# One table for the order of a first up-projection stage (RetNet recurrence, then a SwiGLU block, in fp32 on one core)

## The chip, the core and the metric

The kernel runs on one core of one Trainium2 chip. The metric is the device time of one execution in microseconds (us); lower is better. A core has five engines with a queue each: TensorE (PE, whose weight loads are listed as PEld), VectorE (DVE), ScalarE (ACT), GpSimd (POOL) and SyncE (SP), which here issues every DMA.

## The reference

```python
def _attn_ref(q, k, v):                       # (B,H,S,D) = (4, 8, 768, 64)
    gamma = 1.0 - 2.0 ** (-5.0 - np.arange(H))
    for t in range(S):
        state = gamma[None, :, None, None] * state + einsum('bhd,bhe->bhde', k[:, :, t], v[:, :, t])
        y[:, :, t] = scale * einsum('bhd,bhde->bhe', q[:, :, t], state)

def _moe_ref(x, w_gate, w_val, w_out):        # (3072,512), (512,1536) twice, (1536,512)
    g = x @ w_gate
    silu = g * (1.0 / (1.0 + np.exp(-g)))
    return silu * (x @ w_val) @ w_out

x = attn_out.transpose(0, 2, 1, 3).reshape(B * S, H * D)
return _moe_ref(x, w_gate, w_val, w_out)
```

The three weight matrices arrive as float64 words and are turned into float32 on the chip.

## The kernel before, in words

**Tiling.** The sequence is cut into chunks of 128 positions, and the 24 chunks of all batches are worked in four segments of six chunks (`seg_chunks`; three positions of two sequences). For each segment there is an attention part (scores, mixing, states), an "up" stage (12 blocks `f` of 128 columns of d_ff, gate and value) and a "down" stage (12 blocks times 6 groups of tokens). The attention of segment s+1 is threaded into the down stage of segment s (`down_stage`).

**The first segment is different.** Its attention runs ahead of everything, in the order of the string given to `do(...)` near the end of the kernel. In that string `s` is the scores of a chunk on PE with two masking multiplications on DVE (L356, L362), `m` the mixing (L413, L416) with a copy by ACT (L419), `t` the state update on PE (L396), `g` the decay of the state on ACT (L382), `k`/`q` the scaling of keys and queries on POOL (capital letters: on DVE), `x` the four operand sums on DVE, `w` warm-up products with no result. `scores` takes its two PSUM banks from one pair, 4 and 5, for every chunk, so a chunk's scores cannot be written before the masking of the chunk before has read those banks.

The up stage of the first segment (`up(f)`, L601 on PE) forms the gate and value products with seven products per block in a Strassen-like scheme, each of four matmul records of 128x384 in fp32. Beside them, in the same stage, everything is prepared that the later segments reuse. For each of 24 weight pieces (12 up, then 12 down): a load of raw words (`load_piece`: `U`, L194), the steps `a`, `b`, `c` on ACT (L212, L216, L220), `S` on DVE (L226) and `C` on POOL (L235). For an up piece then `T`, three differences on DVE, and a store of the unit to DRAM (L160). For a down piece then `F` with parts 0 to 3: ACT (L667), POOL (L670), DVE (L673), DVE (L677), which fill one of three `oitem` tiles, and a store (L252).

**What sets the order.** Each block `f` has six places, at which `aside(f, place)` emits side work between two products. Engines run their own instructions in the order of emission, and so does the DMA queue of SP. Before the change the side work of a place comes from three sources: the dictionary `beside`, filled from formulas (`when`, `loads_at`, `todo`), a list `stores` (each store goes out at the start of the place after the one that made it), and events in time (`at`/`run`), which hold the side tables and the first transfers for the next segment:

```python
for i in range(4):
    at(T0 + UP0 * (5.3 + i / 2), load_side, i // 2, i % 2)
for n in range(5):
    at(T0 + UP0 * (7.5, 8.2, 8.8, 9.5, 10.2)[n], load_pair, 1, n)
```

`load_side(g, m)` (L436, L438, L442) brings a half of a side table for the later segments into `tab` (g = 0) or `kept_vk` (g = 1); `load_pair` (L452, L455) brings keys, queries and values. The two gate multiplications of block f-1 (`muls`, L616 and L617 on DVE) stand at a fixed spot in `up(f)`, ahead of the first sum of the block (L633). The transposed loads `U` of pieces share places: the up pieces 2, 5, 8, 11 use the first `rawp` tile, 1, 4, 7, 10 the second, 3, 6, 9 the third; the down pieces use halves of the fourth and of `loads`.

Of the kernel before, what the change touches and what calls it, by code (L numbers as in the profile page):

```python
# [13 lines left out]
U32 = mybir.dt.uint32  # L14
# [35 lines left out]
def tile_retnet_swiglu(  # L50
# [88 lines left out]
    def load_chunk(c, places):  # L139
        for t in places:  # L140
            own = chunks.setdefault(c, [])
            nc.sync.dma_start(out=t, in_=(k_t, q_t, v_n, k_n)[len(own)][c])
            own.append(t)
# [26 lines left out]
    def load_piece(piece):  # L170
# [11 lines left out]
        if wide:  # L182
            t = raw_places[kind].pop(0)
            if kind == "down" or a:
                raw_places[kind].append(t)
            to = raw[piece] = t.bitcast(U32).rearrange("p (a b) -> p a b", a=n)
# [10 lines left out]
    places, stores = [0], []  # L197
# [41 lines left out]
    def three_dn(piece, part):  # L239
        a = piece[1]  # L240
        if part == 0:
            wo[a] = item("o", DM)
        o, x = [wo[a][:, i] for i in range(3)], made[DOWN.index(a) % 5]
        if part == 0:
            far_a(o, x)
        elif part == 1:
            far_b(o, x, pool)
        elif part == 2:
            far_c(o)
        else:  # L250
            far_d(o, True)
            stores.append((places[0], lambda: nc.sync.dma_start(  # L252
                out=w_dn3[a], in_=wo[a].bitcast(U32))))

    def sums_t(piece, parts=range(3)):
# [9 lines left out]
        if parts[-1] == 2:  # L265
            stores.append((places[0], lambda: keep_wt(a)))
# [13 lines left out]
        "U": lambda n: load_next("up"), "D": lambda n: load_next("down"),  # L280
        "F": lambda n, p: three_dn(pieces[n], p[0]),
# [3 lines left out]
    def do(order):  # L285
        for o in order.split():
            n, _, part = o[1:].partition(":")
            parts[o[0]](int(n or 0), *([[int(part)]] if part else []))

    beside = {  # L290
        (0, 0): "c1 S1 C1 U D", (0, 2): "a2 b2", (0, 3): "c2", (0, 5): "T1",
        (1, 0): "a3", (1, 1): "S2 b3 C2 U", (1, 2): "c3", (1, 4): "T2", (1, 5): "S3 C3 U",
    }

    when = [(4, 14, 15, 16, 16, 16), (12, 9, 9, 10, 11, 11, 17, 18)]
    when += [(f + 2, *(6 * f + i for i in (-3 + (f == 3), -2 + (f == 3), -1, 1, 1))) for f in range(3, 10)]
    when += [(f + 10, *(6 * f + i for i in (2, 2, 3, 3, 3, 5, 6))) for f in range(3, 9)]
    when += [(f + 19, *(54 + 2 * f + i for i in (0, 0, 1, 1, 1, 5, 6))) for f in range(5)]
    loads_at = [(16, "U")] + [(6 * f + 1, "U") for f in range(3, 7)]
    loads_at += [(q, "D") for q in (12, 18, 24, 30, 36, 42, 46, 47, 48)]  # L300
    sign_banks.update({3: (4, 6), 12: (7,), 19: (4,), 20: (7,), 21: (6,), 22: (7,), 23: (6,)})
    todo = [(6 * n - 7 if n > 4 else 6 * n - 4 + (n == 3), f"T{n}") for n in range(3, NF)]
    todo += [(53, "k4"), (59, "k5"), (61, "t4"), (66, "t5")]
    for n, *at_ in when:
        sign_banks.setdefault(n, (6, 7) if n < NF else (4,))
        ops = [f"{p}{n}" for p in "abcSC"] + [f"F{n}:0 F{n}:1", f"F{n}:2 F{n}:3"]
        todo += zip(at_, ops)
    order = lambda e: (e[0], "CUD".find(e[1][0]))
    for q, what in sorted(todo + loads_at, key=order):
        key = divmod(q, 6)  # L310
        beside[key] = beside.get(key, "") + " " + what

# [3 lines left out]
    def aside(f, place):  # L316
        places[0] = 6 * f + place
        while stores and (stores[0][0] <= places[0] - 1):
            stores.pop(0)[1]()
        if (f, place) == (7, 5):  # L320
            raw_places["down"][:0] = [hsp[:, ts(i, 1024)] for i in range(2)]
        do(beside.get((f, place), ""))
        run(T0 + UP0 * (f + (place + 1) / 7))

    to_load = {"up": [("up", f) for f in range(NF)], "down": [("down", f) for f in DOWN]}

    raw_places = {"up": [loadp[0][:, :2048], loadp[1][:, :2048], loadp[0][:, :2048],
                         hsp[:, :2048]],
                  "down": [midp[:, ds(0, 1024)], midp[:, ds(1024, 1024)],
                           loads[:, ds(0, 1024)], loads[:, ds(1024, 1024)]]}  # L330

    def load_next(kind):
        if to_load[kind]:
            load_piece(to_load[kind].pop(0))
# [15 lines left out]
    def scores(c):  # L350
        kt, qt = (pairs(t) for t in chunks[c][:2])
# [33 lines left out]
    def state(c):  # L385
# [3 lines left out]
        vn, kd = chunks[c][2:]  # L389
# [44 lines left out]
    def load_side(g, m):  # L434
        cols = decays[:, MASK0:QDEC0].rearrange("p (i g t) -> p i g t", i=2, g=2)[:, :, g]
        nc.sync.dma_start(out=side[g][half[m], :, : 2 * P], in_=cols[half[0]])  # L436
        for i in range(2):
            nc.sync.dma_start(  # L438
# [152 lines left out]
    def up(f):  # L591
# [39 lines left out]
        if f:  # L631
            left.pop(f - 1)[1]()
# [84 lines left out]
    def make_x(t, s, p):  # L717
        soon = p == L - 1
        for m in range(4):
            at(t + 0.4 * m, sum_x, m)  # L720
        when = [(0.2, 1.7, 2.3, 3.0), (0.9, 2.6, 3.0, 3.4), (1.6, 3.5, 4.3, 5.4)] if soon else [
            (0.2, 2.0, 2.6, 3.4), (0.9, 3.2, 3.6, 4.2), (1.6, 3.9, 6.6, 8.0)]
        for (a, b, c, d), n in zip(when, (1, 2, 0)):
            at(t + a, lambda n=n: far_a(*x_part(s, p, n)))
            at(t + b, lambda n=n: far_b(*x_part(s, p, n)))
            at(t + c, lambda n=n: far_c(x_part(s, p, n)[0]))
            at(t + d, lambda n=n: far_d(x_part(s, p, n)[0]))
# [21 lines left out]
    def weights(t, f, g):  # L749
        it = {}  # L750
        if f == 0:
            t -= 1.8
# [5 lines left out]
        at(t - 7.2, begin)  # L758
        at(t - 5.6, lambda: near_b(*it["o"]))
        at(t - 4.4, lambda: near_c(it["o"][0]))  # L760
# [11 lines left out]
    def up3(s, f, t):  # L772
# [9 lines left out]
        e = lambda n: t + (n + 1) * PROD + 0.1  # L782
        at(e(0), copy, p1, x)
        at(e(1), tt, c11, z, p1, op=add)
        at(e(1) + 0.7, act, gate, c11, AF.Silu, scale=ONE)
        at(e(2), copy, u2, x)
        at(e(3), copy, p5, wb)
        at(e(4), tt, hT[:, f, 1], x, p5, op=add)
        at(e(5), tt, hT[:, f, 0], wb, u2, op=add)
        at(e(5) + 0.7, tt, hT[:, f, 0], hT[:, f, 0], gate, op=mul)  # L790
        at(e(6), act, x, x, AF.Silu, scale=ONE)
        at(e(6) + 0.7, tt, hT[:, f, 1], hT[:, f, 1], x, op=mul)
# [5 lines left out]
    def h_split(t, f):  # L798
# [7 lines left out]
        at(t - 7.5, begin)  # L806
        at(t - 6.3, lambda: near_b(it["o"], hT[:, f].rearrange("p i t -> p (i t)")))
        at(t - 5.3, lambda: near_c(it["o"], both))
# [38 lines left out]
    def down_stage(s, t, first_order=range(6), between=None):  # L847
        nxt = s + 1 if s + 1 < NSEG else None
        slot_at, steps = [], []
        for n in range(6 * NF):  # L850
# [4 lines left out]
            if nxt and n in PARTS:  # L855
# [3 lines left out]
                if what == "s":  # L859
                    at(t, scores_of, p, g)  # L860
                    for i in range(2):
                        at(d, decayed, p, g, i)
                    if g and ci:
                        for i in range(2):
                            at(d, scale_q2, p, i)
                elif what == "m":
                    at(t, mix_own, nxt, p)
                    at(d, fence)
                    if ci < NCK - 1:
                        for i in range(2):  # L870
                            at(d, scale_k2, p, i)
                elif what == "o":
# [3 lines left out]
                    for c in range(2):  # L876
                        for i in range(2):
                            for hh in range(2):
# [149 lines left out]
```

## Time and profile before

| what | value |
|---|---|
| time, median of 3 runs | 697.34 us (695.87 to 697.41) |
| the profiled execution: time, span | 697.91 us, 696.1 us |
| granted TensorE clock, mean over the span | 0.994 |
| PE busy | 667.5 us, 96% of the span |
| DVE, ACT, POOL busy | 472.3 us, 383.3 us, 248.9 us |
| first matmul record of the first up stage (L601) | 29.05 us |
| last four records of L601 begin | 154.04 us |
| DMA moved over the span | 141.59 MB, mean 203 GB/s |

Times inside a profile count from the start of the span. The columns of a timeline are: start, length, engine, line, operation, tiles, how many records, and in brackets how long the engine had sat idle before it and what it waited for. "x <- y" in a list of waits reads: the engine and line named first waited for the one named after the arrow. PE is busy nearly everywhere, so the places where it is not, and what it waits for there, matter more than shares of busy time.

### The profile page before, as it was taken

What the parts mean: (1) busy time and instruction counts of PE and PEld (TensorE: products, weight loads), DVE (VectorE), ACT (ScalarE), POOL (GpSimd) and SP (SyncE); (2) the same over time, 40 slices, a digit from 0 to 9 for tenths busy, and PEclk for the clock granted to TensorE, in tenths of its full rate; (3) what the DMA queues carried; (4) which work ended last, traced back from release to release, by engine and by line L of the source; (5) the groups of instructions that cost most, each with busy time, mean ns of one, the idle gap of its engine ahead of it and who ended that gap; (6) DMA issues with size and microseconds to landing.
All of it is one profiled execution on the core that took longest, in us unless ns stands there. A gap on an engine that the chain in (4) does not pass through costs nothing.

```text
span 696.1 us, 12337 instructions
## 1 busy us (share of the span) xinstructions
PE 667.5 (96%) x4724; PEld 549.0 (79%) x4724; DVE 472.3 (68%) x742; ACT 383.3 (55%) x793; POOL 248.9 (36%) x164
## 2 busy tenths in 40 slices
PE   7998999979999999999999899999999999999997
PEld 7754555447677899997677799998777799999886
DVE  3766878955887766665776866666577867667541
ACT  2668689535565555553578554565464655545111
POOL 0434556620111665650100566651011455662000
PEclk9999999999999999999999999999999999999999
DMA  9799959964674543274766443354756553413553
GB/s 319 265 379 319 380 189 345 405 269 152 228 228 176 196 144 121 97 231 149 255 203 228 147 169 106 106 189 158 238 180 209 208 188 113 153 54 106 195 196 139
DMA packets 49515, 141.59 MB, mean 203 GB/s; under 512 B 6064, under 2 KB 18864, under 8 KB 49456
## 3 DMA queue, kind: packets, MB, share of 16 engines
q1 hardware_dynamic: 49456, 140.80, 58.3%
q8 instruction: 37, 0.61, 0.4%
q14 instruction: 22, 0.18, 0.1%
HBM read 114.04 MB, written 26.74 MB: 202 GB/s over the span
## 4 chain that ended last, share of the span: by engine, by line
PE 59%; DVE 17%; ACT 8%; issue 3%; DMA 3%; POOL 0%; DVEq 0%; ACTq 0%; POOLq 0%; SPq 0%
PE bank L768 34%; PE bank L820 14%; PE bank L601 7%; PE bank L458 4%; ACT chunk_x L699 3%; DVE gitem L661 3%; DMA wdnt<-oitem 2%; DVE x L673 2%; DVE x L80 2%; DVE gitem L80 1%; DVE tmp L80 1%; ACT gitem L658 1%; DVE hT L121 1%; DVE tmp L477 1%; DVE chunk_x L831 1%
## 5 line engine op out<-in xcount | busy, mean ns | idle before, releaser
L768 PE MATMUL bank<-x,gitem 128*128 128x384 f32 x1296 | 234.3, 336 | 4.6 <-ACT tmp L121 4.6
L768 PEld LDWEIGHTS bank<-x,gitem 128*128 128x128 f32 x1296 | 225.5, 188 | 8.4 <-ACT tmp L121 7.6
L820 PE MATMUL bank<-oitem,gitem 128*128 128x512 f32 x864 | 214.6, 401 | 0.7 <-DVE gitem L80 0.6
L820 PEld LDWEIGHTS bank<-oitem,gitem 128*128 128x128 f32 x864 | 158.7, 188 | 41.7 <-issue 2.9
L664 POOL TENSOR_TENSOR gitem<-gitem 128x768 fp32r<-128x768 f32 x72 | 136.0, 1889 | 133.7 <-DVE gitem L661 133.7
L601 PE MATMUL bank<-first 128*128 128x384 f32 x336 | 115.1, 501 | 8.5 <-DVE hT L617 3.6
L661 DVE SCALAR_TENSOR_TENSOR gitem<-gitem,loads 128x768 fp32r<-128x768 f32 x72 | 74.1, 1030 | 63.1 <-ACT gitem L658 63.1
L601 PEld LDWEIGHTS bank<-first 128*128 128x128 f32 x336 | 64.1, 194 | 57.5 <-issue 7.4
L661 DVE SCALAR_TENSOR_TENSOR gitem<-gitem,hT 128x768 fp32r<-128x768 f32 x48 | 46.3, 964 | 48.2 <-ACT gitem L658 48.2
L531 POOL TENSOR_TENSOR loads<-loads,tab 128x512 f32<-128x512 f32 x8 | 15.0, 1878 | 157.3 <-PE bank L458 157.3
L658 ACT ACTIVATE gitem<-loads 128x768 fp32r<-128x768 f32 x72 | 60.8, 844 | 0.0
L121 ACT ACTIVATE bank<-bank 128x384 f32<-128x384 f32 x36 | 17.1, 475 | 78.2 <-PE bank L768 78.2
L235 POOL TENSOR_TENSOR first<-first,rawp 128x1024 int32<-128x1024 int32 (+1 forms) x21 | 40.0, 1908 | 42.2 <-DVE first L226 12.7
L658 ACT ACTIVATE gitem<-hT 128x768 fp32r<-128x768 f32 x48 | 39.6, 837 | 25.9 <-PE bank L820 25.8
L121 ACT COPY tmp<-bank 128x384 f32<-128x384 f32 x108 | 51.2, 476 | 2.2 <-PE bank L768 1.9
L121 DVE TENSOR_TENSOR hT<-bank,tmp 128x384 f32<-128x384 f32 x72 | 39.6, 554 | 16.4 <-PE bank L768 16.4
L699 ACT COPY chunk_x<-bank 64x256 f32<-64x256 f32 x72 | 26.5, 368 | 37.4 <-PE bank L458 35.9
L80 DVE SCALAR_TENSOR_TENSOR gitem<-gitem 128x768 fp32r<-128x768 f32 x48 | 45.8, 955 | 1.0
L768 PE MATMUL bank<-x,oitem 128*128 128x384 f32 x216 | 43.9, 339 | 1.3 <-DVE hT L121 1.3
L121 ACT ACTIVATE bank<-tmp 128x384 f32<-128x384 f32 x36 | 17.8, 496 | 48.5 <-DVE tmp L121 48.5
L121 DVE TENSOR_TENSOR hT<-hT,bank 128x384 f32<-128x384 f32 x72 | 39.9, 554 | 4.9 <-ACT bank L121 1.6
L679 ACT ACTIVATE x<-x 128x512 fp32r<-128x512 f32 (+2 forms) x27 | 18.9, 700 | 37.8 <-DVE x L673 37.8
(89 smaller groups left out, 683.3 us busy)
## 6 DMA issues: line engine op xcount, KB each, us to landing
oitem<-wdnt SPq DMA_DIRECT2D x45, 768.0 KB, 4.3
loads<-wup SPq DMA_DIRECT2D x36, 896.0 KB, 4.7
wup<-first SPq DMA_DIRECT2D x12, 896.0 KB, 7.9
wdnt<-oitem SPq DMA_DIRECT2D x12, 768.0 KB, 8.2
rawp<-in_w_val_dram SPq DMA_DIRECT2D x24, 256.0 KB, 5.8
rawp<-in_w_gate_dram SPq DMA_DIRECT2D x12, 512.0 KB, 7.3
out_dram<-chunk_x SPq DMA_DIRECT2D x24, 256.0 KB, 2.1
loads<-in_k_t_dram SPq DMA_DIRECT2D x18, 256.0 KB, 4.2
```

Source lines behind the costliest of these rows:

```text
L80: stt(o, x, 1.0, y, op0=mul, op1=op)
L121: events.append((t, len(events), lambda: fn(*args, **kw)))
L235: pool(d[:, ts(i, n)].bitcast(I32), d[:, ts(i, n)].bitcast(I32), lo[:, ts(i, n)].bitcast(I32), op=add)
L458: nc.tensor.matmul(o, a, b, start=start, stop=True, skip_group_check=True)
L601: nc.tensor.matmul(o, w[:, slot, k], a[:, k], start=(start and k == 0), stop=(stop and k == KH - 1), skip_group_check=True)
L658: act(o[0], x, AF.Copy, scale=CUT / FAR)
L661: stt(o[1], f32(o[0]), -FAR, x, op0=mul, op1=add)
L664: op(o[2], f32(o[0]), f32(o[1]), op=add)
L679: act(o[2], f32(o[2]), AF.Copy, scale=FAR / ONE)
L699: copy(cx[half[i], ds(2 * h, 2), c], y_both(h, i, c))
L768: nc.tensor.matmul(o, w[:, a, k], xs_of[s][:, a, OP[p], k], start=start and a == k == 0, stop=a == 2 and k == KH - 1, skip_group_check=True)
L820: nc.tensor.matmul(banks[tok], hs[f][:, a, ds(i * TH + u * P, P)], wo[f][:, a], start=f == a == 0, stop=f == NF - 1 and a == 2, skip_group ...
```

## The change

All side work of the first segment, the opening included, now stands in one string `START` and one table `beside` of 73 places (six for each of 12 blocks, and one behind them). The letters gain: `l` a load of an attention chunk, `A` a part of the decay table, `U` with its place in memory, `Z` a store, `M` the gate multiplications, `P` a `load_pair`, `L` a quarter of `load_side`, and `T` in single parts. So every one of them has a position of its own. `load_side` issues its wide piece as two DMAs, one for each half `i`, instead of one DMA over both. The numbers of the later stages move into a table `WHEN` with the offsets that the formulas gave (rounded to 0.01). Lines left out are marked "...".

```diff
-    do("""
-        s0 w6 s1 m0 m1 K0 t0 K1 s2 t1 g2 g3 Q2 s3 m2 x0 k2 q3 t2 s4 a0 b0 m3 k3 t3 q4 c0
-        g4 s5 S0 g5 x1 m4 a1 q5 C0 U m5 x2:0 T0:0 x2:1 T0:1 x2:2 x2:3 T0:2 b1 U D D
-    """)
+    START = """
+        l0:0 l0:1 A0 l1:0 l1:1 l0:2 l1:2 A1 l0:3 l2:0 l2:1 l1:3 l2:2 l2:3 l3:0 l3:1 l3:2
+        l3:3 l4:0 l4:1 U0:0 l4:2 l5:0 l5:1 l5:2 l4:3 l5:3 s1 s0 K0 m1 w6 k2 K1 t0 m0 s2 t1
+        g3 Q2 g2 x0:0 x0:1 s3 U1:2 q3 m2 m3 t2 x1:0 k3 a0 x0:2 x0:3 t3 b0 x1:1 s4 S0 q4 x1:2
+        c0 s5 q5 x1:3 m4 C0 m5 a1 x2:0 U3:4 T0:0 x2:1 T0:1 U2:0 T0:2 x2:2 x2:3 U12:6
+    """
...
-    beside = {
-        (0, 0): "c1 S1 C1 U D", (0, 2): "a2 b2", (0, 3): "c2", (0, 5): "T1",
-        (1, 0): "a3", (1, 1): "S2 b3 C2 U", (1, 2): "c3", (1, 4): "T2", (1, 5): "S3 C3 U",
-    }
-    when = [(4, 14, 15, 16, 16, 16), (12, 9, 9, 10, 11, 11, 17, 18)]
...
-    loads_at = [(16, "U")] + [(6 * f + 1, "U") for f in range(3, 7)]
-    loads_at += [(q, "D") for q in (12, 18, 24, 30, 36, 42, 46, 47, 48)]
...
+    beside = """
+        b1 | c1 S1 U13:7 | g5 g4 C1 | a2 T1:0 U14:8 | U15:9 | c2 b2 T1:1 a3 |
+        S2 T1:2 | b3 C2 Z0 S3 | Z1 T2:0 | c12 c3 a12 C3 M0 b12 | U5:0 a13 T2:1 | T2:2 |
+        S12 C12 T3:0 M1 |  | T3:1 F12:0 U4:2 Z2 | T3:2 a4 b4 U6:4 S4 a5 Z3 | F12:1 c4 F12:2
+            C4 | b5 S5 T4:0 |
+        T4:1 c6 L0 | M2 U16:6 c5 C5 | b13 c13 S13 | L1 C13 U7:2 a6 a14 | F12:3 T5:0 U8:0 b6
+            | T4:2 T5:1 S6 F13:0 |
+        F13:1 Z4 F13:2 b14 | F13:3 Z13 C6 M3 S14 | a15 a7 b7 c7 | T5:2 T6:0 T6:1 Z12 | S7
+            T6:2 Z5 L3 c14 b15 | C14 U18:8 F14:0 |
+        S15 C7 F14:1 | M4 F14:2 F14:3 | a8 U9:4 U17:7 Z6 c15 | C15 a16 Z14 | L2 F15:0 T7:0 |
+            F15:1 c8 b8 |
...
+        T10:2 S19 F18:3 M8 a20 | b20 C11 | c20 S20 | a21 b21 T11:0 | a22 S21 C19 C20 | T11:1
+            T11:2 t4 c21 Z18 F19:0 |
+        F19:1 F19:2 k5 F20:0 Z10 F19:3 | b22 F20:1 t5 C21 a23 b23 | F21:0 S22 c22 M9 F21:1
+            Z11 F20:2 | c23 F20:3 C22 Z19 | S23 F22:0 C23 F21:2 | F21:3 Z20 |
+        F23:0 F22:1 Z21 F22:2 | M10 F22:3 Z22 | F23:1 F23:2 |  | F23:3 | |
+        Z23
+    """.split("|")
...
     def aside(f, place):
-        places[0] = 6 * f + place
-        while stores and (stores[0][0] <= places[0] - 1):
-            stores.pop(0)[1]()
...
-        do(beside.get((f, place), ""))
+        do(beside[6 * f + place])
         run(T0 + UP0 * (f + (place + 1) / 7))
...
     def load_side(g, m):
         cols = decays[:, MASK0:QDEC0].rearrange("p (i g t) -> p i g t", i=2, g=2)[:, :, g]
-        nc.sync.dma_start(out=side[g][half[m], :, : 2 * P], in_=cols[half[0]])
         for i in range(2):
+            nc.sync.dma_start(out=side[g][half[m], i, : 2 * P], in_=cols[half[0], i])
             nc.sync.dma_start(
                 out=side[g][half[m], i, 2 * P :].rearrange("p (n t) -> p n t", n=2),
...
@@ up(f)
-        if f:
-            left.pop(f - 1)[1]()
         tt(hT[:, f, 0], wb, u2, op=add)
...
-    for i in range(4):
-        at(T0 + UP0 * (5.3 + i / 2), load_side, i // 2, i % 2)
-    for n in range(5):
-        at(T0 + UP0 * (7.5, 8.2, 8.8, 9.5, 10.2)[n], load_pair, 1, n)
...
+    at(end, do, beside[-1])
+    for n in range(3, 5):
+        at(end + 1.0 + n, load_pair, 1, n)
```

Reading aids for the table: places are counted from 0, six to a block. In the part that is left out stand, among others, P0, P1 and P2 at places 40, 41 and 53 (by their due times they went out at 45, 49 and 53 before), `M10` stands at place 67 (69 before), `U1` in the opening behind the scores of the fourth chunk (before: ahead of the last loads of chunks). `F19`, `F20`, `F21`, `F22`, `F23` begin at places 59, 60, 62, 64, 66 (before: 59, 61, 63, 65, 67); `F12` is spread over places 14 to 22 (before: 17 and 18).

## The prediction

> **What bounds the kernel now.** I read the busy times first, then PE's timeline up to 160 us, because the change rewrites the order of the first segment and only restates the later stages (their offsets are the old ones; the rounding by at most 0.005 us lets no event pass another of its neighbours). The idle brackets of PE are therefore the whole budget.
>
> ```profile
> PE 667.5 (96%) x4724; PEld 549.0 (79%) x4724; DVE 472.3 (68%) x742; ACT 383.3 (55%) x793; POOL 248.9 (36%) x164
> ...
> 30.97 11.88 PE L601 MATMUL bank<-first 128*128 128x384 f32 x36 [0.37 <-DVE first L80]
> 43.47 22.71 PE L601 MATMUL bank<-first 128*128 128x384 f32 x68 [0.62 <-ACT tmp L625]
> 68.96 60.27 PE L601 MATMUL bank<-first 128*128 128x384 f32 x180 [2.77 <-DVE hT L617]
> 133.49 2.85 PE L601 MATMUL bank<-first 128*128 128x384 f32 x8 [0.86 <-ACT tmp L628]
> 137.19 2.99 PE L601 MATMUL bank<-first 128*128 128x384 f32 x8 [0.86 <-DVE hT L617]
> 145.14 7.00 PE L601 MATMUL bank<-first 128*128 128x384 f32 x16 [2.85 <-ACT tmp L620]
> ```
>
> The stage runs from 29.05 us to about 155.1 (its last four records begin at 154.04). The long undisturbed row gives 60.27/180 = 0.335 us a record, so 336 records need 112.5; two state updates (0.64 each) and three L820 records (0.25 each) lie among them: 114.5. The stage takes 126.0, so 11.5 us are lost. The brackets hold 8.9 of it (0.37, 0.62, 2.77, 0.86, 0.86, 2.85 and one of 0.60 behind a gitem); the rest is the slow clock after the two long gaps, seen next.
>
> Where the waits come from is in SP's timeline, in windows, and in ACT's waits from 128 to 152 us:
>
> ```profile
> 89.78 0.72 SPq L436 DMA_DIRECT2D tab<-in_decays_dram  x1
> 95.19 1.26 SPq L438 DMA_DIRECT2D tab<-in_decays_dram  x2
> ...
> 99.82 1.25 SPq L438 DMA_DIRECT2D tab<-in_decays_dram  x2
> ...
> 101.76 0.58 SPq L160 DMA_DIRECT2D wup<-first  x1
> ...
> SPq L438 <- DMA tab<-in_decays_dram: 6.6, 2, 4.6
> ...
> 90.00:100.00 10.00, 10.00 (x32) 5.89 (x31) 7.94 (x16) 8.60 (x15) 5.01 (x3) 1.00 0.47 137
> 110.00:150.00 40.00, 35.41 (x129) 19.55 (x128) 30.98 (x47) 26.30 (x49) 23.86 (x17) 0.96 1.00 378
> ...
> ACT oitem L667 <- DMA wdnt<-oitem: 10.6, 4, 4.2
> ```
>
> Twice the narrow piece of a side table waits until the wide piece has landed, and SP can issue nothing else: 6.6 us. The DMA engines fall to 137 GB/s; the unit store due then leaves at 101.76. From 110 to 150 us they are full (share 1.00), a store of an oitem takes 8 to 11.5 us to land, and ACT waits 10.6 us for an oitem to come free. ACT's queue then holds the copies of L620 to L628 that PE needs. That is the end of the stage. The 2.77 at 68.96 is another thing: F12, S5 and T4 in one row on DVE ahead of L617, with T4 at 3.69 us for three sums that take 1.60 elsewhere without POOL beside them.
>
> **The change part by part.**
>
> *Side tables.* The wait of 6.6 us on SP goes. It costs four more DMAs of about 0.6 us on SP, 2.4 us, hidden while SP waits for C (L194 on POOL, 25.5 us of waiting up to 200 us). L0 and L1 move from places 32 and 35 to 18 and 21, ahead of U16, U7 and U8, where 6 us of waiting would now hurt.
>
> *Tail.* P3 and P4 (1 MB) leave the full stretch and go out behind Z23. The scaling of these keys began at 157.9, and a transfer of the kind landed 7.6 us after issue in the full stretch, so with Z23 at about 150 they are in time; uncovered, this costs up to 4 us. With loads and stores issued when ready, places 54 to 68 carry two unit stores and five oitem stores, 5.7 MB in 24 us, 240 GB/s instead of 378. A store then lands in 5 to 7 us (one wdnt issued at 102.92 took 7.0). F22 at place 64 needs Z19, issued about 4 places (6 us) earlier; F23 at 66 needs Z20, issued 3 places earlier, but comes behind the first copy and both gates of its block. I take 0 to 1 us of wait. M10 comes two places earlier, ahead of the gitem work. So 0.86 + 0.86 + 2.85 and their slow clock (1.7) go, and the 0.60 stays: 6.3 gained.
>
> *Middle.* F12 is spread from place 14 to 22, T4 stands in three places, M2 ahead of them: the 2.77 and its 1.7 of clock go: 4.5 gained. M and Z cost nothing by themselves: the same instructions, elsewhere. By the durations of the rows ACT carries at most 8.6 us in a block of 9.4, DVE 8.7, POOL 8.9, so no engine becomes the bound.
>
> *Early blocks.* U3 now stands ahead of U2 on SP and both wait for the end of the opening. Before, of two up loads issued from 30.22 on, the second landed at 40.3, 10.1 us later. Now U2 is the second: a2 on ACT starts 10.1 us behind the first issue, with a2 itself, c2, b2, a3 (1.05 us each) and then the copy p1 of block 1 in the queue behind it (0.4). U3 goes at about 34.0 (the end of m5's reading), so p1 is done at 34.0 + 10.1 + 3.15 + 1.05 + 0.4 = 48.7; PE needs it 12.6 us into the stage (1.9 and eight products of 1.34), at 47.6: 1.1 of stall, where the old row had 0.62. U4 goes from the first place to behind U5 (issued about 16 us after the opening's end, landing 10 us later), just as ACT reaches a4: between 0 and 2 us, I take 0.3. c6 and c5 stand ahead of p5 and u2 of block 3 and cost 0.2. The stalls of 0.37 stay. Against the old 0.62 this is 1.0 lost. Gains of the stage: 4.5 + 6.3 − 1.0 = 9.8; I take 1.1 off for sums on DVE that meet POOL: 8.7.
>
> *The opening* is where the change loses. PE's rows and the masking on DVE:
>
> ```profile
> 4.77 1.25 PE L356 MATMUL bank<-hT 64*128 64x128 f32 x16
> 5.95 1.60 PE L909 MATMUL bank<-warm 128*128 128x128 f32 x12
> 8.73 1.16 PE L356 MATMUL bank<-hT 64*128 64x128 f32 x16 [1.18 <-DVE tmp L362]
> ...
> 16.13 1.16 PE L356 MATMUL bank<-hT 64*128 64x128 f32 x16 [1.31 <-DMA hT<-in_q_t_dram]
> ...
> 23.87 1.16 PE L356 MATMUL bank<-rawp 64*128 64x128 f32 x16 [0.47 <-DMA rawp<-in_q_t_dram]
> ...
> 7.36 1.29 DVE L362 TENSOR_TENSOR tmp<-bank,tab 128x512 f32<-128x512 f32 x2 [6.36 <-DMA tab<-in_decays_dram]
> ```
>
> The reader is to see that before, s0 is done while the mask is still under way, s3 and s5 start when their queries land, and little else holds PE. Now s1 stands first. Its queries, issued at 2.59, landed 6.0 us later, so PE stands still from 4.8 to 8.65, and s0 cannot start until both maskings of s1 have freed the two banks. In order, with 1.16 for scores, 1.25 for a pair of maskings, 2.05 for a mixing with state (1.02 without), 0.64 for a state and 1.6 for w6: s1 8.65 to 10.8 (at half clock, below), masked by 12.1; s0 to 13.3; m1, w6, t0, m0, s2, t1 to 19.4; s3 waits for the masking of s2, 20.0 to 21.2; m2, m3, t2 to 26.0; t3 waits for the sum of t2 on DVE, to 27.0; s4 to 28.2, its masking (behind x0:2, x0:3, x1:1 on DVE) at 29.7; s5 29.7 to 30.9; m4 and m5 to 35.0. C0, behind q5 on POOL, ends at 34.7. So the stage begins at 35.0 and not at 29.05: 6.0 lost. From below: the PE work alone from 8.65 on is 21.1 us, 29.8, so 0.7. From above: 8.2, by the rule now weighed.
>
> *The clock.* These are windows of two us around the first long gap:
>
> ```profile
> 66.00:68.00 2.00, 0.18 (x1) 0.00 (x0) 1.97 (x3) 1.75 (x3) 1.13 (x1) 1.00 0.84 219
> 68.00:70.00 2.00, 1.04 (x3) 0.68 (x4) 2.00 (x5) 0.00 (x0) 0.00 (x0) 0.96 1.04 420
> 70.00:72.00 2.00, 2.00 (x4) 0.96 (x3) 1.97 (x4) 0.67 (x2) 1.28 (x1) 0.50 1.00 325
> 72.00:74.00 2.00, 2.00 (x6) 1.10 (x5) 1.97 (x3) 0.82 (x3) 1.39 (x1) 0.69 1.07 387
> ```
>
> After 2.77 us of idle PE the granted clock is 0.50 from 69.84 to 73.24 (in windows of one us), and again from 144.92 to 148.34: 3.4 us each, 22 periods of 3.413 apart. The Trainium skill, "TensorE: Matmul & The Clock Gate", § Part 1: The HAM clock gate, says that a free-running window of 3.413 us decides, that an idle window halves the clock and that about one busy window restores it. It speaks against this change. Counted back from 69.84, windows begin at 4.99 and 8.40: the new idle stretch fills one. By the trace's case (restored after one window) only s1 is slow, 1.16 becoming about 2.15 (warm-up records took 0.237 cold against 0.133): 1.0 lost, in the 6.0 above. By the rule taken strictly, a window only two thirds busy may not restore it, and s0, m1 and part of w6 run slow too: 8.2. I take the trace's.
>
> *Sum.* 6.0 − 8.7 = −2.7 us. The profiled execution took 697.91 (its span and 1.8 around it), 0.57 above the median of 697.34. The change taken off the median gives 694.6 us; off the execution's own time, 695.2.
>
> **The rivals.** *Slower: the ping-pong of the two score banks in the opening.* Same place, 4.8 to 35 us; it decides from the point where the stage wins back less than the opening loses. For it: PE is in order, and every step of it is a wait that the profile already shows once. Against: DVE and ACT are lightly loaded there, and steps may close up. With 8.2 lost and half of the old 11.5 still lost (5.7 gained) it is +2.5: 699.8. *The opening is harmless, near 0.7 to 2 lost*, and the stage gains 9 to 10: −8, 689. Against it: the bank wait was 1.2 us already at 8.73. *The tables change nothing:* the wait of L438 is not one of overlap. The pieces for kept_vk, of the same shape, went out at 107.98 and 108.72 without a wait, so overlap in memory alone does not explain it. Then SP waits at places 18 and 21, the tail keeps half its stalls, 3 less gained: 697.6.
>
> **How the numbers follow.** My sum 0.5 (692.5 to 697), harmless opening 0.13, tables without effect 0.12, slower rival 0.25. About 0.3% (2.1 us) is what a measurement can tell from none. Faster by more: 0.4 of the first, all of the second: 0.53; slower: most of the rival and a little of the third, 0.23; 0.24 between. The range leaves out the outer parts of the second and fourth: 689.5 to 700.
>
> **What would show it.** Right: first L356 near 8.7 with some 3.9 idle before it, clock 0.50 in 8.4 to 11.8, first L601 near 35, the last near 152.4; no wait of L438 on tab; ACT's wait on wdnt under 2; no granted 0.50 between 40 and 150. Wrong: first L601 before 32 (opening mis-sized), or a gap of over 2 us in the stage, above all at a2 or a4 for rawp.

## The result, and the profile after

The changed kernel takes 694.89 us (median of 20 runs), the kernel before 697.37 us (median of 20): a ratio of 0.9965 with a 95% interval of 0.9952 to 0.9977, or 2.5 us less. One of the 20 runs of the changed kernel took 931.83 us, far outside the others (693.0 to 698.7), and is not in the ratio. The profiled execution took 693.57 us, with a span of 691.8 (before: 697.91 and 696.1).

Line numbers have moved: L601 is now L663, L356 is L418, L413 and L416 are L475 and L478, the gate multiplications L616 and L617 are L678 and L679, the two additions that follow them in a block (L633, L636) are L693 and L696, L677 is L737, L667 is L727, L235 is L232, L194 is L191, L438 is L500.

First PE's timeline of the changed kernel, in the opening and in the stage (start, length, what, and in brackets the idle time ahead of it):

```profile
1.05 3.78 PE L963 MATMUL bank<-warm 128*128 128x128 f32 x16 [1.05 <-DVE warm L967]
9.03 2.08 PE L418 MATMUL bank<-hT 64*128 64x128 f32 x16 [4.20 <-DMA hT<-in_q_t_dram]
11.85 2.67 PE L418 MATMUL bank<-hT 64*128 64x128 f32 x16 [0.74 <-DVE tmp L424]
14.45 1.95 PE L478 MATMUL bank<-tmp,hT 128*64 128x128 f32 x16
16.34 1.60 PE L963 MATMUL bank<-warm 128*128 128x128 f32 x12
...
36.57 1.56 PE L663 MATMUL bank<-first 128*128 128x384 f32 x4
38.39 10.59 PE L663 MATMUL bank<-first 128*128 128x384 f32 x32 [0.26 <-DVE first L80]
49.40 19.65 PE L663 MATMUL bank<-first 128*128 128x384 f32 x60 [0.43 <-ACT tmp L682]
69.34 14.57 PE L663 MATMUL bank<-first 128*128 128x384 f32 x44 [0.29 <-ACT tmp L687]
86.15 44.50 PE L663 MATMUL bank<-first 128*128 128x384 f32 x136 [2.24 <-DVE hT L696]
...
135.88 14.46 PE L663 MATMUL bank<-first 128*128 128x384 f32 x44
```

Two things are to be seen. The stage starts at 36.57 us where it started at 29.05: 7.5 us lost. And in the stage four short idle times are left, 3.2 us together, where there were 8.9. Its last four records are followed by the next instruction on PE at 151.87 us (155.14 before), so the stage takes 115.3 us instead of 126.1: 10.8 us won. The idle time accounts for 5.7 of that, and the two stretches of half clock, which this execution does not have (mean granted clock 1.000, before 0.994), for 3.4. The other 1.7 is not assigned. The two together give −3.3 at 152 us; the rest of the difference between the spans (−4.3) comes after 310 us, where both kernels run the same instructions.

The first matmuls also show something that the clock row of the page does not. The scores of the second chunk took 2.08 us and the mixing 1.95; the same instructions take 1.16 and 1.09 later. Those of the first chunk took 2.67; in their new place they take 1.75 at full speed (the run with more warm-up, below), because the second of their two banks comes free later. PE ran at half speed until about 16.3 us. The page's clock row stands at 9 in every slice all the same: the record of the granted clock in the trace has its first entry, full clock, at 16.26 us, and what lies ahead of it counts as full. At the start, the duration of one record is what tells the clock: here 2.08/16, against 1.16/16.

Next SP's timeline where the side tables go out, and the DMA engines in the windows in which they had been empty, then full (us, busy time and count of PE, PEld, DVE, ACT and POOL, granted clock, DMA share, GB/s):

```profile
63.11 0.56 SPq L499 DMA_DIRECT2D tab<-in_decays_dram  x1
63.71 1.50 SPq L500 DMA_DIRECT2D tab<-in_decays_dram  x1
65.26 0.62 SPq L499 DMA_DIRECT2D tab<-in_decays_dram  x1
65.93 0.62 SPq L500 DMA_DIRECT2D tab<-in_decays_dram  x1
...
90.00:100.00 10.00, 10.00 (x32) 5.89 (x31) 8.68 (x13) 8.47 (x15) 6.25 (x4) 1.00 0.98 355
110.00:150.00 40.00, 40.00 (x153) 23.38 (x151) 38.09 (x60) 29.87 (x55) 26.64 (x19) 1.00 0.88 354
```

The four pieces leave within 3.4 us, none waits for another, and from 90 to 100 us the engines move 355 GB/s instead of 137. Between 30 and 152 us ACT never waits for the store of an oitem (10.6 us before). PE works through all of the last 40 us.

What is new is the gap at 86.15. DVE's timeline ahead of it, with POOL's rows of the same time:

```profile
78.76 2.52 DVE L737 TENSOR_SCALAR oitem<-oitem 128x512 fp32r<-128x512 f32 x1
...
83.20 2.43 DVE L80 SCALAR_TENSOR_TENSOR first<-first 128x256 f32<-128x256 f32 x3
85.55 0.54 DVE L696 TENSOR_TENSOR hT<-bank,tmp 128x384 f32<-128x384 f32 x1
...
78.26 2.74 POOL L232 TENSOR_TENSOR first<-first,rawp 128x1024 int32<-128x1024 int32 x1 [1.94 <-DVE first L223]
83.77 1.58 POOL L232 TENSOR_TENSOR first<-first,loads 128x512 int32<-128x512 int32 x1 [2.77 <-ACT loads L217]
```

PE waits for the addition L696 at 85.55, which stands behind three sums of 2.43 us (1.60 without POOL beside them) and, further up the queue, behind the scaling L737: 2.52 us, ending 0.3 us after POOL's C of piece 6 (78.26 to 81.00). All twelve L737 in one line (count, then shortest, median and longest in ns), the same line before the change, L677, below it:

```profile
L737 DVE TENSOR_SCALAR oitem<-oitem x12: 408/1074/2525, 72.8 to 150.2; 128x512 fp32r<-128x512 f32 x12
```

```profile
L677 DVE TENSOR_SCALAR oitem<-oitem x12: 426/427/429, 62.7 to 150.0; 128x512 fp32r<-128x512 f32 x12
```

Before, the scaling stood right behind L673, which waits for POOL's part of the same F, and in no case was it stretched. In the table it meets POOL at work: eight of the twelve are stretched, and each of these ends 0.28 or 0.29 us after an operation of POOL ends.

### The profile page after: what moved, and what is told of

Read it like the earlier page. It is cut to its first block, busy times and chain, and to the rows that moved or that the text cites. A ratio compares the mean times of both kernels' runs of the same rounds, so it can differ in the third digit from the quotient of the medians.

```text
span 691.8 us, 12321 instructions
## 1 busy us (share of the span) xinstructions
PE 666.2 (96%) x4724; PEld 551.0 (80%) x4724; DVE 474.9 (69%) x742; ACT 382.5 (55%) x793; POOL 250.3 (36%) x164
## 4 chain that ended last, share of the span: by engine, by line
PE 64%; DVE 17%; ACT 9%; issue 4%; DMA 3%; SPq 1%; POOL 0%; DVEq 0%; ACTq 0%; POOLq 0%
PE bank L824 34%; PE bank L874 14%; PE bank L663 9%; PE bank L520 4%; ACT chunk_x L759 4%; DVE gitem L721 3%; DVE x L733 2%; DVE x L80 2%; DMA rawp<-in_w_gate_dram 2%; DVE tmp L80 1%; DVE gitem L80 1%; PE bank L418 1%; ACT gitem L718 1%; DVE chunk_x L885 1%; DVE tmp L539 1%
## 5 line engine op out<-in xcount | busy, mean ns | idle before, releaser
L663 PE MATMUL bank<-first 128*128 128x384 f32 x336 | 110.9, 489 | 3.2 <-DVE hT L696 2.2
L663 PEld LDWEIGHTS bank<-first 128*128 128x128 f32 x336 | 62.8, 190 | 49.4 <-DVE hT L696 3.1
L232 POOL TENSOR_TENSOR first<-first,rawp 128x1024 int32<-128x1024 int32 (+1 forms) x21 | 41.4, 1975 | 34.4 <-DVE first L223 17.9
L824 PEld LDWEIGHTS bank<-x,oitem 128*128 128x128 f32 x216 | 36.8, 188 | 3.2 <-DVE hT L841 2.3
L724 POOL TENSOR_TENSOR oitem<-oitem 128x256 fp32r<-128x256 f32 x36 | 28.6, 794 | 15.2 <-DVE oitem L721 13.5
L520 PEld LDWEIGHTS bank<-loads 64*64 64x64 f32 (+1 forms) x800 | 22.6, 134 | 13.8 <-issue 5.1
```

The source lines that it names most:

```text
L232: pool(d[:, ts(i, n)].bitcast(I32), d[:, ts(i, n)].bitcast(I32), lo[:, ts(i, n)].bitcast(I32), op=add)
L520: nc.tensor.matmul(o, a, b, start=start, stop=True, skip_group_check=True)
L663: nc.tensor.matmul(o, w[:, slot, k], a[:, k], start=(start and k == 0), stop=(stop and k == KH - 1), skip_group_check=True)
L724: op(o[2], f32(o[0]), f32(o[1]), op=add)
L824: nc.tensor.matmul(o, w[:, a, k], xs_of[s][:, a, OP[p], k], start=start and a == k == 0, stop=a == 2 and k == KH - 1, skip_group_check=True)
```

## The experiments

"Before" beside these runs was 696.97 to 697.69 us. Each ratio is to it, with its 95% interval. In the kernels with the old opening the lines are one lower (L662 for L663).

### The old order of the opening, the rest of the change kept

```diff
-        ... s1 s0 K0 m1 w6 k2 K1 t0 m0 s2 t1
-        g3 Q2 g2 x0:0 x0:1 s3 U1:2 q3 m2 m3 t2 x1:0 k3 a0 x0:2 x0:3 t3 b0 x1:1 s4 S0 q4 x1:2
-        c0 s5 q5 x1:3 m4 C0 m5 a1 x2:0 U3:4 ...
+        ... s0 w6 s1 m0 m1 K0 t0 K1 s2 t1 g2 g3
+        Q2 s3 U1:2 m2 x0 k2 q3 t2 s4 a0 b0 m3 k3 t3 q4 c0 s5 S0 x1 m4 q5 C0 m5 a1 x2:0 U3:4 ...
```

> The changed kernel, with the order of PE, DVE, ACT and POOL in the opening put back to that of the kernel before (s0 w6 s1 ...); the loads, the table of places and the split side tables stay. Theory (the opening costs 7.5 us in the profile, 36.57 against 29.05 for the first product, and all of it lies on PE's path): the first product of the up stage is back at 29 to 29.5 us, the stage keeps its 115.7 us, and the time falls by 6.5 to 7.5 us below the changed kernel, to about 687.5. Rival (the late opening gave loads and conversions a lead that the new table needs): the first product is at 29, but gaps of 2 to 4 us appear in the blocks 1 to 5, and the gain is 3 to 4 us, 691.

Measured: 688.31 us, 0.9861 [0.9842, 0.9881]. That is 6.6 us under the changed kernel, and the lowest median of all the kernels here. PE's timeline of it:

```profile
28.88 1.56 PE L662 MATMUL bank<-first 128*128 128x384 f32 x4
...
79.54 46.17 PE L662 MATMUL bank<-first 128*128 128x384 f32 x136 [2.25 <-DVE hT L695]
```

So the new opening costs 6.6 us and everything else in the change brings 9. The gap ahead of the 136 records is the one just described, 6.6 us earlier; here the clock was at half from 80.3 to 83.8 behind it.

### The changed kernel with eight warm-up products ahead of the first scores

```diff
-        ... l4:3 l5:3 s1 s0 K0 m1 w6
+        ... l4:3 l5:3 w8 s1 s0 K0 m1 w6
```

> The changed kernel, with eight more warm-up products ahead of s1, so that PE is busy while it waits for the queries of s1; the order of the opening stays. Theory (the clock takes part of the loss: s1, s0 and m1 ran at half speed up to about 16.3 us): s1 in 1.2 us instead of 2.1, s0 and m1 likewise, the first product 2 to 2.5 us earlier, at about 34.3; time 692.5. Rival (all of the loss is the wait for the banks and for DVE, and the slow matmuls hide in it): the first product stays within 0.7 us of 36.6, time 694.5 to 695.

Measured: 692.45 us, 0.9918 [0.9904, 0.9932], 2.4 us under the changed kernel. Its first rows on PE:

```profile
8.47 1.16 PE L418 MATMUL bank<-hT 64*128 64x128 f32 x16 [1.41 <-DMA hT<-in_q_t_dram]
...
33.32 1.56 PE L663 MATMUL bank<-first 128*128 128x384 f32 x4
```

Useless products in the idle time keep PE warm: the scores take 1.16 instead of 2.08 and the stage starts 3.25 us earlier. Of this, 0.56 is only that the queries landed sooner in this execution (8.47 against 9.03); the three slow rows give the other 2.7. So the clock is about 2.4 of the 6.6. What is left is order.

### The old first two scores in front, the rest of the new opening kept

```diff
-        ... s1 s0 K0 m1 w6 k2 K1 t0 m0 s2 t1
+        ... s0 w6 s1 K0 m1 k2 K1 t0 m0 s2 t1
```

> The changed kernel with s0 w6 s1 K0 m1 in front of the opening, as before, in place of s1 s0 K0 m1 w6; all that follows (s3 and s4 late, m2 m3 t2 t3 ahead of s4) stays as changed. Theory (the first half of the loss is s1 first: cold clock, and s0 behind the banks; the second half is s4 and s5 behind four mixings and the masking): s3 at about 16.5, the first product at 31 to 32 us, time 690 to 691.5. Rival (the first two steps are all of the loss): first product at 29 to 29.8, time 688 to 689. Other rival (what follows sets the end): first product after 34, time above 692.5.

Measured: 689.26 us, 0.989 [0.9872, 0.9907], with the first product at 30.52. This takes back 5.6 of the 6.6: nearly all of the loss is that the chunk whose queries land later stands first, and that the warm-up products stand behind it and not in the wait. The rest of the new order costs about 1 us by the medians, less than was expected of it, and the intervals of this run and of the one with the old opening overlap.

### The kernel before with the split of the side tables alone

```diff
-        nc.sync.dma_start(out=side[g][half[m], :, : 2 * P], in_=cols[half[0]])
         for i in range(2):
+            nc.sync.dma_start(out=side[g][half[m], i, : 2 * P], in_=cols[half[0], i])
```

> The kernel before, with nothing changed but load_side, whose wide piece goes out as two DMAs. Theory (the wait of SP for the tab pieces is one of overlapping boxes, and the 6.6 us set the full stretch from 110 us on): no wait of the narrow piece; the DMA share of 90 to 100 us rises from 0.47 to over 0.8, ACT's wait for wdnt falls from 10.6 to under 6 us, the time falls by 1.5 to 4 us, to 693.5 to 696. Rival (the tail is full because of where stores and transfers of keys stand, not because of 6.6 us on SP): the wait goes, the tail keeps its gaps, time within 1 us of before.

Measured: 694.22 us, 0.9948 [0.9933, 0.9963]: 3.3 us under before. SP's timeline, a window, and ACT's wait in the last stretch:

```profile
90.35 0.61 SPq L437 DMA_DIRECT2D tab<-in_decays_dram  x1
91.01 0.65 SPq L438 DMA_DIRECT2D tab<-in_decays_dram  x1
...
98.22 0.53 SPq L160 DMA_DIRECT2D wup<-first  x1
...
90.00:100.00 10.00, 10.00 (x32) 5.89 (x31) 7.93 (x16) 8.60 (x15) 5.00 (x3) 1.00 0.74 238
...
ACT oitem L667 <- DMA wdnt<-oitem: 8.5, 3, 4.1
```

The unit store leaves at 98.22 instead of 101.76, so the engines move 238 GB/s from 90 to 100 us instead of 137. But ACT still waits 8.5 us for oitem tiles, and PE's idle time in the stage is 8.75 us, as before (8.9). The split gains, but it is not what took away the waits at the end, and the path by which it gains is not shown. The stage is 3.1 us shorter in this profile than in that of before, but this execution has no half clock in the stage, where the one of before has two stretches worth 3.4 us; the theory's path, a share above 0.8 and a wait under 6 us, was missed.

### The changed kernel with the old, merged side tables

```diff
+        nc.sync.dma_start(out=side[g][half[m], :, : 2 * P], in_=cols[half[0]])
         for i in range(2):
-            nc.sync.dma_start(out=side[g][half[m], i, : 2 * P], in_=cols[half[0], i])
```

> The changed kernel with load_side as before (the wide piece in one DMA over both halves). Theory: SP waits again, 2 to 5 us each at L0 and L1 (63 and 68 us), U16, U7, U8 go out 4 to 7 us later, and the time rises by 0.5 to 3 us above the changed kernel, to 695.5 to 698, through a7 or a8 on ACT. Rival (the loads have enough slack at their new places): the waits are back, but the time stays within 0.5 us, 694.5 to 695.4.

Measured: 699.17 us, 1.0024 [1.0014, 1.0033], 4.3 us more than with the split, and more than was expected. Without the split the whole change would be a loss. SP's wait, its rows, and PE's:

```profile
SPq L500 <- DMA tab<-in_decays_dram: 8.6, 2, 5.3
...
62.70 0.72 SPq L498 DMA_DIRECT2D tab<-in_decays_dram  x1
68.75 1.25 SPq L500 DMA_DIRECT2D tab<-in_decays_dram  x2
...
75.31 1.25 SPq L500 DMA_DIRECT2D tab<-in_decays_dram  x2
...
77.70 0.89 SPq L191 DMA_DIRECT2D rawp<-in_w_val_dram  x2
...
91.59 31.59 PE L663 MATMUL bank<-first 128*128 128x384 f32 x92 [3.36 <-ACT tmp L682]
```

The wait comes with the merged piece: the narrow ones then stand for 8.6 us in all. That the two pieces overlap in the tile fits, but is not shown to be the reason; pieces of the same shape for `kept_vk` did not wait before. Behind them in SP's queue stands the load of piece 7, which leaves at 77.70 instead of 71.47. ACT waits 5.2 us for it, and PE waits 3.36 us for ACT, with half the clock for 3.4 us. The side table itself is first read at 160.9 us. The price is the traffic queued behind it.

### The split, and F12 spread forward

```diff
-    when = [(4, 14, 15, 16, 16, 16), (12, 9, 9, 10, 11, 11, 17, 18)]
+    when = [(4, 14, 15, 16, 16, 16), (12, 9, 9, 10, 11, 11, 14, 15)]
```

> The kernel before with the split side tables, and the four steps of F12 at places 14 and 15 instead of 17 and 18, ahead of S5 and T4; all else as before. Theory (the gap of 2.76 us in block 4 is F12, S5 and T4 in a row on DVE, begun late since F12 waits on POOL behind C4): the gap falls to under 1 us, with or without a slow clock behind it, and the time falls by 2 to 3.5 us, to 690.7 to 692.2. Rival (T4 at 3.7 us beside POOL is enough by itself): the gap stays above 2 us, 693.5 to 694.5.

Measured: 692.09 us, 0.9933 [0.991, 0.9957]. This is 2.1 us under the split alone by the medians, though the two intervals overlap. PE's rows:

```profile
61.28 64.14 PE L601 MATMUL bank<-first 128*128 128x384 f32 x196 [0.42 <-ACT tmp L620]
...
133.84 4.42 PE L601 MATMUL bank<-first 128*128 128x384 f32 x8 [2.45 <-DVE hT L617]
```

The gap of 2.77 near 69 us is gone, and up to 125 us nothing longer than 0.85 us (at 58 us) has come in its place. It was the row of F12, S5 and T4 on DVE. The gap in the last stretch stays.

### The last two transfers of keys, put early again and put late alone

In the changed kernel P3 and P4 go back to places 57 and 61. In the kernel with the split alone they go behind the stage.

```diff
-        ... | a21 b21 T11:0 | ... | b22 F20:1 t5 C21 a23 b23 | ...
+        ... | a21 b21 T11:0 P3 | ... | b22 F20:1 t5 C21 a23 b23 P4 | ...
...
-    for n in range(3, 5):
-        at(end + 1.0 + n, load_pair, 1, n)
```

> The changed kernel with P3 and P4 back at the places 57 and 61, where they stood before, instead of behind the end of the stage. Theory (they helped to fill the tail of the stage): stores of oitem land 1 to 2 us later, ACT waits 0 to 2 us for wdnt, 0 to 1.5 us more time, 694.9 to 696.4. Rival (with the stores spread the DMA engines have room, and where they stand is worth nothing): within 0.5 us of the changed kernel.

```diff
-        at(T0 + UP0 * (7.5, 8.2, 8.8, 9.5, 10.2)[n], load_pair, 1, n)
+        at((T0 + UP0 * (7.5, 8.2, 8.8)[n]) if n < 3 else end + 1.0 + n, load_pair, 1, n)
```

> The kernel before with the split side tables, and P3 and P4 behind the end of the stage as in the changed kernel; all else as before. Theory (1 MB less between 130 and 150 us lets the stores land sooner): ACT's wait for wdnt falls from 8.5 to 4 to 6 us and the time by 0.5 to 2 us, to 692.2 to 693.7. Rival (it is the places of the oitem steps that make the waits): ACT's wait stays at 8 us, time within 0.5 us of the split alone, 694.2.

Measured: 695.32 us, 0.9969 [0.9955, 0.9983], and 694.87 us, 0.9961 [0.9946, 0.9976]. The first is 0.4 us above the changed kernel, the second 0.65 above the split alone, and neither can be told from no difference. ACT's wait for oitem tiles moves much as the theories had it:

```profile
ACT oitem L727 <- DMA wdnt<-oitem: 2.6, 1, 2.6
```

This is the first of the two; the changed kernel has no such wait. With the transfers late in the other kernel the wait is 6.2 us instead of 8.5, and PE still has a gap of 2.49 near 138 us. So a megabyte less in the full stretch takes some 2.5 us off ACT's waits, and nothing that shows off the time.

### Closing the gaps that are left

Four kernels on top of the old opening try to better the 688.31. First, three sums moved from place 27 behind the addition that PE waited for, and U2 ahead of U3:

```diff
-        ... | a15 a7 b7 c7 | T5:2 T6:0 T6:1 Z12 | S7
-            T6:2 Z5 L3 c14 b15 | C14 U18:8 F14:0 |
+        ... | a15 a7 b7 c7 | Z12 | S7
+            T5:2 Z5 T6:0 L3 c14 b15 | T6:1 T6:2 C14 U18:8 F14:0 |
```

> The kernel with the old opening order, with two more edits: the three sums T5:2, T6:0 and T6:1 move from place 27 to places 28 and 29 (behind the addition of L696 for which PE waited 2.25 us), and U2 goes to SP ahead of U3 (a2 on ACT waited for it, then PE 1.40 us). Theory: both gaps go, and with the first one a stretch of half clock (80.3 to 83.8 us, 1.7 us): 3 to 5 us below the kernel with the old opening alone, 684 to 685.5. Rival (the gap at the addition is made by L737, held for 2.5 us beside POOL, and by L223 behind it, and not by the sums): the gap stays above 1 us and moves to the copies, 686.5 to 688.

Measured: 688.98 us, 0.9875 [0.9851, 0.9899]. No gain. The gap of L695 is gone from its place, but it has moved:

```profile
84.55 18.41 PE L662 MATMUL bank<-first 128*128 128x384 f32 x56 [1.64 <-ACT tmp L686]
```

Two of the sums now stand beside POOL's C14 and C7, take 3.26 us, and hold the addition L698 on DVE. A gate on ACT needs that one, and the copy that PE waits for stands behind the gate. Another gap, of 1.48, came near 60 us, where a4 waits for U4.

Second, the scaling in another form of instruction:

```diff
-            nc.vector.tensor_scalar(o[2], f32(o[2]), FAR / ONE, None, op0=mul)
+            stt(o[2], f32(o[2]), FAR / ONE - 1.0, f32(o[2]), op0=mul, op1=add)
```

> The kernel with the old opening order, with the last scaling of a down piece (L737, a tensor_scalar on DVE) written as a scalar_tensor_tensor of the tile with itself (the factor less one, times it, plus it). Theory (a tensor_scalar on DVE stands still while a tensor_tensor of POOL runs: L737 took 0.41 to 2.53 us, and ended just after POOL; the other form only slows down): no instance of the line above 1.7 us, 0.69 alone, the gap of 2.25 us in block 4 falls below 1.2 us, the time by 1 to 3 us below the old opening alone, to 685.5 to 687.3. Rival (any DVE operation with its input and output in SBUF waits for POOL alike): the line still takes over 2 us beside POOL, the gap stays, and 12 times 0.26 us are added on DVE: 688.3 to 689.5.

Measured: 691.11 us, 0.9913 [0.9889, 0.9937]: 2.8 us more. The line's answer:

```profile
L736 DVE SCALAR_TENSOR_TENSOR oitem<-oitem x12: 674/1341/2782, 67.8 to 147.9; 128x512 fp32r<-128x512 f32 x12
```

The other form is held by POOL too (2782 ns) and takes 0.26 us more where POOL leaves it alone. The 2.8 us are not all its price: in the profile the first product of the stage comes at 31.49 instead of 28.88, since PE waited 2.83 us for queries and the clock was then at half, and the stage itself is no longer than with the old scaling. The same form, with U2 ahead of U3 and U4 right behind Z0, is the third:

```diff
-        S2 T1:2 | b3 C2 Z0 S3 | ... | T3:1 F12:0 U4:2 Z2 | ...
+        S2 T1:2 | b3 C2 Z0 U4:2 S3 | ... | T3:1 F12:0 Z2 | ...
```

> The old opening order, the scaling as a scalar_tensor_tensor, U2 on SP ahead of U3, and U4 on SP right behind the first unit store instead of behind U5. Theory: a2 and a4 on ACT no longer wait for their loads (gaps of 1.40 and 1.48 us go), and the gap of block 4 is below 1.2 us: no gap above 1.2 us and no half clock in the stage, 2 to 4 us below the old opening alone, 684.3 to 686.3. Rival (waits only move to the next queue, as with the sums): within 1 us of 688.3.

Measured: 690.55 us, 0.9907 [0.9891, 0.9923]. The waits of a2 and a4 are gone; the gap at 80.42 stays at 2.39 us, and so does the slower scaling.

Fourth, with the old scaling, S6 moved from place 23 to place 25, behind the scaling of F13, so that POOL's C6 starts later:

```diff
-            | T4:2 T5:1 S6 F13:0 |
-        F13:1 Z4 F13:2 b14 | F13:3 Z13 C6 M3 S14 | ...
+            | T4:2 T5:1 F13:0 |
+        F13:1 Z4 F13:2 b14 | F13:3 S6 Z13 C6 M3 S14 | ...
```

> The kernel with the old opening order, with S6 on DVE moved from place 23 to place 25, behind the last step of F13, so that C6 on POOL, which waits for S6, begins after that step and cannot hold it. Theory (the 2.5 us of the scaling in block 4 is DVE held by C6, and the gap of 2.25 us on PE follows from it): the scaling takes 0.43 us there, C6 starts 1 us later, the gap falls below 1.2 us and the half clock behind it goes, 1.5 to 3.5 us below the old opening alone, 684.8 to 686.8. Rival (C6 then holds the sums T5:2, T6:0 and T6:1 instead): the gap stays above 1.8 us, 687.5 to 689.

Measured: 689.04 us, 0.9873 [0.9851, 0.9894]. The scaling, a store on SP, a row of ACT, two rows of PE, and a window (columns as above):

```profile
72.22 0.43 DVE L736 TENSOR_SCALAR oitem<-oitem 128x512 fp32r<-128x512 f32 x1
...
102.57 0.33 SPq L160 DMA_DIRECT2D wup<-first  x1
...
111.92 1.12 ACT L209 ACTIVATE first<-rawp 128x1024 f32<-128x1024 f32 x1 [2.14 <-DMA wup<-first]
...
44.23 67.19 PE L662 MATMUL bank<-first 128*128 128x384 f32 x204 [1.48 <-ACT tmp L681]
113.46 13.57 PE L662 MATMUL bank<-first 128*128 128x384 f32 x36 [2.05 <-ACT tmp L689]
...
110.00:120.00 10.00, 7.95 (x20) 4.21 (x20) 7.30 (x13) 6.28 (x10) 4.73 (x3) 0.83 1.02 419
```

This shows the mechanism of the gap: C6 now starts at 73.97, behind the scaling, which takes 0.43 us instead of 2.5, and the gap is gone; PE runs 67 us without a bracket. Yet no time is won. PE arrives earlier at block 10, and there another wait is met. The up units live in a ring of four places (`ring[f % 4]`), so step `a` of piece 11 cannot write before the unit of piece 7 has been stored. That store was issued at 102.57 and landed 9.3 us later, with the DMA engines full from 90 to 120 us; the raw words of piece 11 had landed by 104.75. ACT waits 2.14 us for the store, PE 2.05 for ACT, and the clock halves. (The stage also began 1.4 us later in this execution than with the old opening alone, by queries that landed later; 5 runs against 4, with medians 0.7 us apart, cannot tell the two kernels apart.)

### The sum of the parts

By medians: before 697.5; the split alone, 694.2 (−3.3); with F12 early, 692.1 (−2.1); with the rest of the table and the old opening, 688.3 (−3.8); with the new opening, 694.9 (+6.6). Medians of one kernel scatter by about 1 us, so the steps are good to about that.

## Why the prediction was right

The time, 694.6, was met within 0.3 us. That is better than its steps were, and so in part luck: both large terms were too small, the opening by 1.5 us and the stage by 2.1 in the profile, and they stand with opposite signs.

- **The opening, 6.0 lost: the place and the cause right, the size too small.** Measured 7.5 in the profile and 6.6 in time (first L601 at 36.57, not near 35). The first scores start at 9.03, near the 8.65 computed. The step that failed is the choice made on the clock. The trace of before showed a half clock that ended after one window, and so only s1 was taken as slow. The rule of the Trainium skill ("TensorE: Matmul & The Clock Gate", § Part 1: The HAM clock gate), taken strictly, had s0, m1 and part of w6 run slow too, and 8.2 lost. At half speed s0 took 2.67 instead of 1.75, m1 1.95 instead of 1.09, and w6 its full-speed 1.60, so the strict reading was the nearer one except for w6. The clock's record agrees with it: counted back from its first entry at 16.26, a window from 9.43 to 12.85 us that PE's rows fill to 2.7 of 3.41 us did not bring the full clock; the next one, filled, did. The half clock that was to be seen in 8.4 to 11.8 is not in the record, which has nothing ahead of 16.26. Warming PE brought 2.4 us back.
- **Where the opening's loss lies.** The ping-pong of the score banks over all six chunks was thought to add up. The first two steps alone, with the warm-up products that stand between them, are 5.6 of the 6.6.
- **The stage, 8.7 gained: measured 10.8 in the profiled execution.** This execution flatters the change. It lies 1.3 us under the median, and its gap of 2.24 us happened not to halve the clock, where one of 2.25 us did with the old opening. One reading was wrong without harm to the sum: the row of 0.335 us a record was called undisturbed, though the half clock from 69.84 to 73.24 lies in it. Without one a record takes 0.327 (44.50/136 after), so the stage needs 112.0 us and not 114.5, and 14.0 us were lost, not 11.5.
- **Side tables: right.** The waits of L438 are gone, at no visible price for the four more DMAs. The rival, by which SP would wait at the new places too, falls: no piece waits there, and merging the pieces again brings the wait back, with 4.3 us. That the pieces for `kept_vk` did not wait before is not explained by this, so what in the merged piece makes the wait stays open.
- **Tail, 6.3: the amount is there, the reason given for it is not.** The transfers P3 and P4 were to leave the full stretch and bring it from 378 to 240 GB/s. It still moves 354, and the two experiments on P3 and P4 found some 2.5 us of ACT's waits and nothing in the time. The late transfers kept ACT waiting 2.15 us at 156.9, and PE did not stand for it. ACT's waits for oitem tiles are indeed gone. Neither the split, nor F12, nor P3 and P4 with the split, does it, by runs that keep 6 to 9 us of these waits, so most of it must lie among the other placements (F19 to F23, the stores at once, gates earlier, traffic drawn forward to 90 to 110 us). Which of them was not separated.
- **Middle, 4.5: the cause right, the gain given back.** F12 in one row was the gap, as the run with F12 alone shows. "No granted 0.50 between 40 and 150" held in the profiled execution, but a gap of over 2 us, named as a sign of error, did come, at 86.15. It is not at a2 or a4, where it was looked for, but at an addition (L696), from DVE operations that POOL holds. The 1.1 set aside for sums that meet POOL was the right worry at half its size (2.24 here, and half clock besides with the old opening).
- **Early blocks, 1.0 lost: not seen.** The gaps are 0.26, 0.43 and 0.29, no more than the old ones. The stall computed for a2, 1.1, measured 0.43; with the old opening it is 1.40.
- **The slower rival** was wrong on the stage only: with a loss of 6.6 to 7.5 its opening was the better estimate, but nothing like half of the old loss was left behind it.

## What to carry to other kernels

A DMA that waits on another piece of its own destination costs what stands behind it in the in-order queue: cut transfers so that none waits for another, and price the next load, not the wait. At the start of a kernel, put first what lands first, and fill the wait with products that keep PE warm; here two swapped steps undid more than half of what 73 ordered places had won (5.6 of 9 us). When a gap closes, look at what the earlier arrival meets before counting the gain: of the tries at the same 2.3 us, the two that closed it met another wait, one on DVE again and one for a store.

## What the runs showed of the hardware

- **A scaling on DVE is held until POOL's operation ends.** A tensor_scalar of 128x512 takes 0.43 us, and 2.52 when it starts 0.5 us behind a 2.74 us tensor_tensor on POOL. All eight stretched ones of the changed kernel end 0.28 or 0.29 us after an operation of POOL; written as scalar_tensor_tensor (up to 2.78), all eight end 0.55 or 0.56 after one. Moved out of POOL's way the scaling takes 0.43 again. Operations of DVE that read a PSUM bank (L678, L679) were not stretched beside POOL (0.54 to 0.56).
- **A cold start can be invisible in the clock row.** After 3.8 us of warm-up (0.24 us a record, against 0.13 later) and 4.2 us of idle PE ran at half speed to about 16.3 us, with nothing in the row. Two more profiles with this opening have their first clock entry at 16.0 (merged side tables) and 17.4 us (P3 and P4 early).
- **The same gap may or may not halve the clock, by where it lies.** An idle time of 2.24 us did not (changed kernel) and one of 2.25 did (old opening); one of 2.75 did and one of 2.76 did not, in two kernels that hold the same split. The traces tell why. The clock of each execution changes only at multiples of 3.413 us from its own first change: with the old opening at 5.25, 80.34 (22 windows later) and 83.75. On this grid the gap of 2.25 (77.29 to 79.54) lies inside one window (76.93 to 80.34), and the half clock follows at that window's end. The gap of 2.24 (83.91 to 86.15) is cut by a border at 84.53 into 0.62 and 1.62; the one of 2.76 (67.73 to 70.50) by one at 68.81 into 1.08 and 1.69. Over the gaps of 2 us and more in the up stages of all the profiles, the eleven with 2.05 us or more inside one window halved the clock, and the five with at most 2.01 did not. No run moved a gap on purpose, and the opening, with its smaller products, does not keep to these figures (with the split alone, 1.80 us of a gap in one window were enough). As the grid lies elsewhere in every execution, this makes part of the scatter between them.
